# One core, attention and two expert stages: the dense stage's first turn by eight block products, and the groups' token numbers and shares kept in DRAM as rows

## The chip, the core and the metric

The kernel runs on one core of a Trainium2 chip. The metric is the device time of one execution in microseconds (us), the median of three runs. A profile is one further execution, recorded by the hardware.

A core has five queues of instructions, each worked off in order: TensorE (PE; its weight loads are shown apart as PEld), VectorE (DVE), ScalarE (ACT), GpSimd (POOL) and SyncE (SP), which here issues nearly all DMAs. They wait for each other through semaphores. An instruction that waits holds all that stands behind it on its engine.

## What is computed

```python
# attention: 4 batches, 8 heads, 576 tokens, 64 wide; causal, window of 128, linear bias
attn = softmax(q @ k.T / 8 + bias, masked) @ v              # -> x, 2304 tokens x 512
# first expert stage: 8 experts, each takes 288 tokens, greedily by the largest logit
logits = x @ w_gate                                         # 2304 x 8
for idx in argsort(-logits.flatten()): assign the token if it is free and the expert has room
for e in range(8): y[mask_e] = relu(x[mask_e] @ w1[e]) @ w2[e]        # 512 -> 1024 -> 512
# second, dense stage: 4 experts, every token through each
p = probs / (probs.sum(-1) + 1e-9)
out = sum(p[:, e] * (relu(y @ w1_e) @ w2_e) for e in range(4))
```

All is float32. A product of two float32 matrices is made of three PE passes over a high and a low part of each operand (`mm3`: high x high, high x low, low x high).

## The kernel before

**Attention** comes first, tokens in 18 tiles of 128. Its rows, with the token's four shares behind the 512 values, go to `x_dram`.

**The grouped stage** follows: eight groups g = 0 to 7 of 288 tokens. For each group a routing chain on DVE and PE (`count`, `enough`, `any`, `narrow`, six rounds, then `who` to `whole`) finds the expert and the token numbers `idx` (96 x 3); POOL gathers the tokens' rows from `x_dram` into `xg`; PE turns them (`rows`, tiles `tp`), and then multiplies by the expert's weights (`hp_a`, then `y`). The weights come in 16 pieces of 128 x 512 (`raw_a`), with five buffers: SP loads a piece (`load_piece`, L745), ACT rounds it to the high part (`wh_a`, L753), DVE makes the low part (`wl_a`, L758). While a group's own work runs, the routing of the next one is in progress, interleaved on DVE and PE. PE time that would be free is filled with a part of the dense stage, expert 0's first 768 hidden columns (`hp_f`, `po_f`, `pt`; partial sums go to `part_dram`).

The step `keep` (L946 to L950) stores a group's token numbers and its shares for later use: `id_dram` has one 4-byte number for each token and `p_dram` four shares, and both are written from tiles whose 96 partitions are tokens, so each token is a piece of its own. `shares_of` (L1035, L1040) reads shares back tile by tile for `pt`; after the last group `ids` and `pp` are read for the dense stage (L1269, L1271).

The order of this stage is set by `arranged` (L1207): each `step` has an engine, an assumed duration, its needs with lags and a rank, and a list scheduler puts them in an order that then is each engine's program order.

**The dense stage** makes 7 units of hidden columns for 3 pairs of token chunks (2 x 384 tokens), 21 turns. A turn's first matmul (512 deep) is cut in halves of depth, hidden columns and tokens, and done by seven products of sums of blocks in place of eight (`first_products`, L1303): x and w1 blocks are added and subtracted beforehand (`token_work`, L1095, on DVE: tiles `b`, `t`; `weight_work`, L1137, on POOL: tiles `a`, `s`) and each of the seven results split in high and low (`xh`/`xl`, `wh`/`wl`). The products land in PSUM tiles `m`; four of the results need further additions on DVE (`u`, `cs`, with a copy `s` by ACT). While the turn's products run, the second matmul of the turn before is interleaved (`po`, with weights `vh`, `vl` from `w2raw`), and the operands of the next turn are prepared; a number called slot says behind which product. The first turn has no turn before it: its operands are prepared at the end of the grouped stage (step `turn`, L1196) and no second matmul lies between its products. After `fctx` closes (L1264) only PE and ACT keep the written order; DVE, POOL and SP instructions of the dense stage are ordered by the framework's own scheduler.

Of the kernel before, what the change touches and what calls it, by code (L numbers as in the profile page):

```python
# [19 lines left out]
P = 128  # L20
# [5 lines left out]
def fused_kernel(ctx: ExitStack, tc: tile.TileContext, q, k, v, w_gate, w1, w2, probs, m2w1, m2w2, out, dbg=None):  # L26
# [25 lines left out]
    id_dram = dram.tile([NT, 1], I32, name="id_dram")  # L52
    p_dram = dram.tile([NT, E2], F32, name="p_dram")
# [470 lines left out]
    moe = ctx.enter_context(tc.tile_pool(name="moe", bufs=1))  # L524
    ps_y = ctx.enter_context(tc.tile_pool(name="ps_y", bufs=2, space=PSUM))
# [389 lines left out]
    for g in range(E):  # L915
# [29 lines left out]

        def keep(g=g):  # L946
            gs = slice(g * CAP, (g + 1) * CAP)
            nc.sync.dma_start(id_dram[gs, :].rearrange("(j i) o -> i (j o)", i=CB), grp[g]["idx"])
            nc.sync.dma_start(p_dram[gs, :].rearrange("(j i) e -> i j e", i=CB), grp[g]["xg"][:, :, DM:])
        step(("keep", g), SP_, 1.2, keep, [(("gather", g), 10.0), (("rows", g, NK - 1), 1.0)], 2)  # L950
# [80 lines left out]
        def shares_of(g=g):  # L1031
            p0 = g * CAP
            fill[g]["p"] = [fw.tile([P, E2], F32, tag="ppf", name=f"ppf_{g}_{t}", bufs=3) for t in range(FULL)]
            for t in range(FULL):
                nc.sync.dma_start(fill[g]["p"][t], p_dram[p0 + t * P : p0 + (t + 1) * P, :])  # L1035
            if g % GR == GR - 1:
                pr = fw.tile([P, E2], F32, tag="ppr", name=f"ppr_{g}")
                for j in range(GR):
                    r0 = (g - GR + 1 + j) * CAP + FULL * P
                    nc.sync.dma_start(pr[j * REM : (j + 1) * REM, :], p_dram[r0 : r0 + REM, :])  # L1040
                fill[g]["p"].append(pr)
# [53 lines left out]
    def token_work(pair):  # L1095

        raw, out, todo = {}, [None] * 7, []
# [17 lines left out]
        def split(i, a, needs):  # L1115
            def up():
                out[i] = [dp["w"].tile([P, 2, CH], F32R, tag=f"x{n}", name=f"x{n}{i}_{pair}", bufs=7) for n in "hl"]
# [3 lines left out]
            return len(todo) - 1  # L1121

# [11 lines left out]
        split(6, (1, 1), [t3])  # L1134
        return todo, out

    def weight_work(u, key):  # L1137
# [41 lines left out]
        l = {ik: load(*ik) for ik in ((0, 0), (1, 0), (1, 1), (0, 1))}  # L1179
# [16 lines left out]
    step(("turn",), SP_, 0.0, late_pools, [("first h", E - 1, NFF - 1, NK - 1), ("fl", E - 1, NFF - 1), ("out", E - 1), ("keep", E - 1), ("gather", E - 1)], 1)  # L1196
    first, begins, later = {}, [], []
    for what, (todo, made) in (("t", token_work(0)), ("w", weight_work(0, "0"))):
        first[what] = made
        begins += [(slot, i, what, todo) for i, (*_, slot) in enumerate(todo) if slot < 7]  # L1200
        later += [(slot, fn) for _, _, fn, _, slot in todo if slot >= 7]
    for n, (slot, i, what, todo) in enumerate(sorted(begins, key=lambda b: b[:3])):
        eng, us, fn, needs, _ = todo[i]
# [215 lines left out]
```

## Time and profile before

| | us |
|---|---|
| three runs | 1252.45, 1257.78, 1258.47 |
| median | 1257.78 |
| the profiled execution | 1262.0 |
| its span, first to last instruction | 1260.3 |
| attention, up to | about 157 |
| routing of the first group, up to | about 200 |
| grouped stage, up to | about 615 |
| change over to the dense stage, up to | about 655 |
| dense stage, up to | 1260.3 |

The profile has a page (busy time of each engine, the span in 40 slices, DMA queues, the chain that ended last, costliest groups of instructions) and a trace that can be asked for the instructions of a stretch in order of time. In these a row gives the start from the span's beginning, the duration, the engine, the line, the operation and its tiles; what stands in brackets is how long the engine had been idle just before and what released it. PEclk is the clock granted to TensorE: 1.00 is 2.4 GHz, 0.50 is 1.2 GHz.

### The profile page before, as it was taken

Reading aid. Unit: us, or ns where it says so; the run is one execution under the profiler, and the core shown is the slowest. Engines: PE = TensorE matmul, PEld = TensorE weight load, DVE = VectorE, ACT = ScalarE, POOL = GpSimd, SP = SyncE. Lnnn points to the kernel's source line nnn. Section 1 sums busy time; section 2 is a strip of 40 time slices with the busy share of each in tenths; the row PEclk is TensorE's granted clock in tenths of the full one; section 3 lists DMA queues with packets and bytes.
Section 4 is the critical chain, followed back from the end, with each engine's and each line's share of the span. In section 5 each row is a group of like instructions: output and inputs, shape, how many; then the busy total and the mean of one; then the engine's idle time right before and its main releaser. Section 6 shows DMA issues by size and latency. Waiting matters only on the chain.

```text
span 1260.3 us, 22074 instructions
## 1 busy us (share of the span) xinstructions
PE 1193.8 (95%) x7975; PEld 1078.0 (86%) x7975; DVE 786.2 (62%) x2048; ACT 525.1 (42%) x1284; POOL 516.8 (41%) x499
## 2 busy tenths in 40 slices
PE   7999926989999999999979999999999999999997
PEld 6998825979898899999968988888888898898886
DVE  6999887868887675442564544764444584454443
ACT  8998733333333334443443333333333342333320
POOL 8867601101000100000487766446664635676622
PEclk9999957989999999999989999999999999999999
DMA  9663144454454525651462322233222113232101
GB/s 180 147 148 85 44 151 112 121 110 132 105 113 101 139 86 145 117 150 20 143 211 59 100 67 68 63 104 118 68 59 59 51 43 109 60 100 68 51 25 51
DMA packets 140734, 122.29 MB, mean 97 GB/s; under 512 B 77648, under 2 KB 104784, under 8 KB 140624
## 3 DMA queue, kind: packets, MB, share of 16 engines
q1 hardware_dynamic: 137648, 111.40, 34.2%
q0 software_dynamic: 2976, 9.48, 2.3%
q8 instruction: 63, 1.03, 0.4%
q14 instruction: 47, 0.39, 0.1%
HBM read 101.88 MB, written 18.96 MB: 96 GB/s over the span
## 4 chain that ended last, share of the span: by engine, by line
PE 72%; DVE 6%; issue 4%; DMA 3%; POOL 2%; ACT 1%; SPq 0%; POOLq 0%; DVEq 0%
PE po L779 8%; PE po L780 8%; PE po L778 8%; PE m L780 7%; PE m L779 7%; PE m L778 7%; PE hp_a L778 3%; PE y L778 3%; PE hp_a L779 2%; PE hp_a L780 2%; PE y L780 2%; PE y L779 2%; DMA raw_a<-in_moe_w_dram 2%; PE hp_f L778 2%; PE hp_f L780 2%
## 5 line engine op out<-in xcount | busy, mean ns | idle before, releaser
L1292 DVE SCALAR_TENSOR_TENSOR acc<-po,pp,acc 128x512 f32<-128x512 f32 x126 | 94.4, 749 | 185.1 <-PE po L780 184.7
L778 PE MATMUL m<-xh,wh 128*128 128x384 f32 x546 | 184.6, 338 | 8.1 <-ACT s L1338 5.6
L780 PE MATMUL m<-xh,wl 128*128 128x384 f32 x546 | 185.8, 340 | 0.0
L779 PE MATMUL m<-xl,wh 128*128 128x384 f32 x546 | 185.7, 340 | 0.0
L779 PE MATMUL po<-vl,hh 128*128 128x512 f32 x468 | 185.2, 396 | 0.0
L780 PE MATMUL po<-vh,hl 128*128 128x512 f32 x468 | 185.2, 396 | 0.0
L778 PE MATMUL po<-vh,hh 128*128 128x512 f32 x468 | 184.7, 395 | 0.0
L1164 POOL TENSOR_TENSOR wl<-a,wh 128x512 fp32r<-128x512 f32 (+1 forms) x114 | 145.3, 1279 | 74.4 <-ACT wh L1162 74.2
L721 POOL DMA_INDIRECT xg<-x_dram,idx x24 | 25.1, 1045 | 362.9 <-PE hp_a L780 144.7
L787 ACT ACTIVATE hh<-cs 128x384 fp32r<-128x384 f32 x117 | 60.8, 525 | 205.4 <-DVE cs L1326 205.4
L1177 POOL TENSOR_TENSOR vl<-w2raw,vh 128x512 fp32r<-128x512 f32 x70 | 95.4, 1365 | 95.5 <-ACT vh L1174 95.5
L1162 ACT CAST wh<-a 128x512 fp32r<-128x512 f32 (+1 forms) x114 | 66.3, 583 | 142.3 <-POOL a L1155 91.6
L778 PEld LDWEIGHTS m<-xh,wh 128*128 128x128 f32 x546 | 104.0, 190 | 14.2 <-ACT s L1338 6.0
L779 PEld LDWEIGHTS m<-xl,wh 128*128 128x128 f32 x546 | 103.7, 190 | 5.7
L780 PEld LDWEIGHTS po<-vh,hl 128*128 128x128 f32 x468 | 87.9, 188 | 20.9
L780 PEld LDWEIGHTS m<-xh,wl 128*128 128x128 f32 x546 | 103.8, 190 | 0.0
L778 PEld LDWEIGHTS po<-vh,hh 128*128 128x128 f32 x468 | 87.8, 188 | 15.9
L779 PEld LDWEIGHTS po<-vl,hh 128*128 128x128 f32 x468 | 88.0, 188 | 15.7
L753 ACT CAST wh_a<-raw_a 128x512 fp32r<-128x512 f32 x128 | 73.5, 620 | 31.3 <-DMA raw_a<-in_moe_w_dram 31.2
L758 DVE TENSOR_TENSOR wl_a<-raw_a,wh_a 128x512 fp32r<-128x512 f32 x128 | 85.1, 681 | 1.3 <-ACT wh_a L753 0.3
L778 PE MATMUL hp_a<-xh,wh_a 128*128 128x288 f32 x256 | 81.8, 320 | 0.1
L790 DVE SCALAR_TENSOR_TENSOR hl<-cs,hh 128x384 fp32r<-128x384 f32 x117 | 73.8, 640 | 11.8 <-ACT hh L787 5.9
(241 smaller groups left out, 3047.6 us busy)
## 6 DMA issues: line engine op xcount, KB each, us to landing
raw_a<-in_moe_w_dram SPq DMA_DIRECT2D x128, 256.0 KB, 3.2
w2raw<-in_moe_w_dram SPq DMA_DIRECT2D x70, 256.0 KB, 2.7
a<-in_moe_w_dram SPq DMA_DIRECT2D x64, 256.0 KB, 3.1
x_dram<-x SPq DMA_DIRECT2D x18, 258.0 KB, 2.7
y_dram<-ys SPq DMA_DIRECT2D x8, 576.0 KB, 3.7
b<-y_dram SPq DMA_DIRECT2D x12, 384.0 KB, 4.3
acc<-part_dram SPq DMA_DIRECT2D x6, 768.0 KB, 5.8
k<-in_k_dram SPq DMA_DIRECT2D x16, 256.0 KB, 4.6
```

The costliest lines, as they stand in the source:

```text
L721: G.indirect_dma_start(out=xg[:, j, :], out_offset=None, in_=x_dram[:, :], in_offset=bass.IndirectOffsetOnAxis(ap=d["idx"][:, j : j + 1], ...
L753: S.copy(res[n][0][0][:, a, b], raw)
L758: V.tensor_tensor(lo[:, a, b], raw, hi[:, a, b].bitcast(F32), ALU.subtract)
L778: T.matmul(o, ah, bh, start=first, stop=False, **kept)
L779: T.matmul(o, ah, bl, start=False, stop=False, **kept)
L780: T.matmul(o, al, bh, start=False, stop=last, **kept)
L787: S.activation(h[0][:, f, :n], hp[:, :n], AF.Relu)
L790: V.scalar_tensor_tensor(h[1][:, f, :n], hp[:, :n], 0.0, h[0][:, f, :n].bitcast(F32), ALU.max, ALU.subtract)
L1162: S.copy(out[i][0], raw[a])
L1164: todo.append((POOL_, 1.3, lambda: G.tensor_tensor(out[i][1], raw[a], out[i][0].bitcast(F32), ALU.subtract), [len(todo) - 1], i))
L1177: todo.append((POOL_, 1.3, lambda: G.tensor_tensor(second[f][1], raw["w", f], second[f][0].bitcast(F32), ALU.subtract), [len(todo) - 1], 8 ...
L1292: V.scalar_tensor_tensor(accs[ch][:, i, :], po, pe, accs[ch][:, i, :], ALU.mult, ALU.add)
```

## The change

Two things change. **Rows in DRAM.** One DRAM tensor `kp_dram` with five rows (the token numbers and the four shares) takes the place of `id_dram` and `p_dram`. For each group ACT packs numbers and shares into a tile `pk` (96 x 15), PE turns it (`pkt`, 15 x 96), ACT copies it to `pks`, and one DMA writes 15 rows of 96 numbers. After the last group one DMA reads all back as 90 rows of 128 (`kt`), PE turns them (`ktt`), ACT copies them to `pp`, and DVE makes the whole numbers `ids` from it. `shares_of` reads one share for a token in place of four.

**The first turn.** For the first turn alone the seven products become eight, of plain blocks (`block_products`): four results, each a sum of two block products in one PSUM tile, so that no `s`, `u` or `cs` is made and only 4 + 4 blocks must be split before the turn. The sums of token blocks that the later turns of the pair need are made behind or during the turn; the sums of weight blocks are not made for this unit. The next unit's weights are prepared in earlier slots (`EARLY`). In later pairs one token operand moves from slot 5 to slot 6.

```diff
-    id_dram = dram.tile([NT, 1], I32, name="id_dram")
-    p_dram = dram.tile([NT, E2], F32, name="p_dram")
+    kp_dram = dram.tile([1 + E2, NT], F32, name="kp_dram")
...
+    pp = moe.tile([P, 1 + E2, NTL], F32, name="pp")
...
+        KR = (1 + E2) * NB
+        def pack(g=g):
+            pk = d["pk"] = rsm.tile([CB, 1 + E2, NB], F32, tag="pk", name=f"pk_{g}")
+            S.copy(pk[:, 0, :], d["idx"])
+            S.copy(pk[:, 1:, :].rearrange("p e j -> p j e"), d["xg"][:, :, DM:])
+        def packed_t(g=g):
+            grp[g]["pkt"] = ps_h.tile([P, 512], F32, tag="h", name=f"pkt_{g}")
+            T.transpose(grp[g]["pkt"][:KR, :CB], grp[g]["pk"].rearrange("p e j -> p (e j)"), ident[:CB, :CB])
+        def packed(g=g):
+            S.copy(grp[g]["pks"], grp[g]["pkt"][:KR, :CB])
         def keep(g=g):
-            nc.sync.dma_start(id_dram[gs, :].rearrange("(j i) o -> i (j o)", i=CB), grp[g]["idx"])
-            nc.sync.dma_start(p_dram[gs, :].rearrange("(j i) e -> i j e", i=CB), grp[g]["xg"][:, :, DM:])
-        step(("keep", g), SP_, 1.2, keep, [(("gather", g), 10.0), (("rows", g, NK - 1), 1.0)], 2)
+            nc.sync.dma_start(kp_dram[:, g * CAP : (g + 1) * CAP].rearrange("e (j i) -> e j i", i=CB), grp[g]["pks"])
+        step(("pack", g), ACT_, 0.5, pack, [(("gather", g), 10.0), (("rows", g, NK - 1), 1.0), (("keep", g - 1), 4.0) if g else None], 2)
+        step(("packed t", g), PE_, 0.2, packed_t, [("pack", g), ("rows", g, NK - 1), bank(banks_h, 4, ("packed", g))], 2)
+        step(("packed", g), ACT_, 0.25, packed, [("packed t", g), (("keep", g - 1), 4.0) if g else None], 1)
+        step(("keep", g), SP_, 0.6, keep, [("packed", g)], 2)
+        if g == E - 1:
+            def by_tiles():
+                nc.sync.dma_start(d["kt"], kp_dram.rearrange("e (t p) -> (e t) p", p=P))
+            def tiles_t():
+                T.transpose(grp[E - 1]["ktt"][:, :KRT], grp[E - 1]["kt"], ident[:KRT, :KRT])
+            def tiles():
+                S.copy(pp.rearrange("p e t -> p (e t)"), grp[E - 1]["ktt"][:, :KRT])
...
-                nc.sync.dma_start(fill[g]["p"][t], p_dram[p0 + t * P : p0 + (t + 1) * P, :])
+                nc.sync.dma_start(fill[g]["p"][t], kp_dram[1, p0 + t * P : p0 + (t + 1) * P].rearrange("(p o) -> p o", o=1))
...
+        if pair == 0:
+            l = {kj: load(*kj) for kj in ((0, 1), (1, 1), (0, 0), (1, 0))}
...
+            for i, kj in ((7, (0, 1)), (6, (1, 1)), (0, (0, 0)), (2, (1, 0))):
+                split(i, kj, [l[kj]])
+            todo[:] = [(*t[:4], 0) for t in todo]
+            t3 = less("t3", (1, 1), (0, 1), ALU.subtract, [], 7)
+            less((0, 1), (0, 1), (0, 0), ALU.subtract, [], 7)
+            less((0, 0), "t3", (0, 0), ALU.add, [], 7)
...
+        if key == "0":
+            for i, ik in ((0, (0, 0)), (2, (0, 1)), (3, (1, 0)), (5, (1, 1))):
+                split(i, ik, [l[ik]])
+            todo[:] = [(*t[:4], 0) for t in todo]
+            for f in range(nf):
+                second_piece(f)
+            return todo, (out, second)
...
-    nc.sync.dma_start(ids, id_dram.rearrange("(t p) o -> p (t o)", p=P))
-    nc.sync.dma_start(pp, p_dram.rearrange("(t p) e -> p t e", p=P))
+    V.tensor_copy(ids, pp[:, 0, :])
...
+    def block_products(u, pair, w, x, h, key):
+        wb = {(0, 0): w[0], (0, 1): w[2], (1, 0): w[3], (1, 1): w[5]}
+        xb = {(0, 0): x[0], (1, 0): x[2], (1, 1): x[6], (0, 1): x[7]}
+        for i, j, bank in ((0, 1, 1), (0, 0, 2), (1, 1, 3), (1, 0, 1)):
+            for f in range(nh):
+                for k in range(2):
+                    for c in range(2):
+                        mm3(m[:, :CH], a[0][:, c, fs], a[1][:, c, fs], b[0][:, c, :], b[1][:, c, :], k == c == 0, k == c == 1)
+                hid_up(m, h[j], i * nh + f, CH)
+                hid_lo(m, h[j], i * nh + f, CH)
...
+    EARLY = (0, 0, 0, 2, 2, 7, 7, 7, 8, 9, 10, 11, 12)
...
-                work += [(slot, fn) for _, _, fn, _, slot in todo]
+                work += [(EARLY[slot] if n == 0 else slot, fn) for _, _, fn, _, slot in todo]
...
-        for i, _ in enumerate(first_products(u, pair, w[0], x, h, str(n))):
+        for i, _ in enumerate((first_products if n else block_products)(u, pair, w[0], x, h, str(n))):
```

What the planner and the framework's scheduler make of it is seen in the order of instructions. The first place is SP in group 1, from the weight piece ahead of `keep` on (`idx` and `xg` are the group's numbers and gathered rows, `raw_a` weight pieces, `pt` partial sums).

Before:

```order
L745 DMA raw_a_1_1_0_5056<-in_moe_w_dram 128x512
L948 DMA id_dram<-idx_4828 96x3x1
L949 DMA p_dram<-xg_4837 96x3x4
L745 ISA
L745 DMA raw_a_1_2_0_5087<-in_moe_w_dram 128x512
L1070 DMA part_dram<-pt_0_5085 128x512
L745 ISA
L745 DMA raw_a_1_3_0_5115<-in_moe_w_dram 128x512
L1070 DMA part_dram<-pt_1_5147 128x512
```

After:

```order
L746 DMA raw_a_1_1_0_5059<-in_moe_w_dram 128x512
L965 DMA kp_dram<-pks_5081 5x3x96
L746 ISA
L746 DMA raw_a_1_2_0_5099<-in_moe_w_dram 128x512
L1107 DMA part_dram<-pt_0_5097 128x512
L746 ISA
L746 DMA raw_a_1_3_0_5124<-in_moe_w_dram 128x512
L1107 DMA part_dram<-pt_1_5159 128x512
```

Two DMAs became one, at the same place in front of the weight pieces 1_2 and 1_3.

The second place is ACT in the same group, from the last turned tile of tokens on (`tp`, `xh`).

Before:

```order
L937 CAST xh_5023<-tp_3_5047 128x288
L753 CAST wh_a_1_4966<-raw_a_1_2_0_4972 128x512
L753 CAST wh_a_1_4966<-raw_a_1_3_0_4997 128x512
L1063 ACTIVATE pt_0_5085<-po_f_0_4984,ppf_0_4475 128x512
L753 CAST wh_a_1_5096<-raw_a_1_0_0_5036 128x512
L753 CAST wh_a_1_5096<-raw_a_1_1_0_5056 128x512
L1063 ACTIVATE pt_1_5147<-po_f_1_5073,ppf_1_4476 128x512
```

After:

```order
L938 CAST xh_5022<-tp_3_5045 128x288
L953 CAST pk_5067<-idx_4832 96x3
L954 COPY pk_5067<-xg_4839 96x3x4
L754 CAST wh_a_1_4966<-raw_a_1_2_0_4964 128x512
L962 COPY pks_5081<-pkt_5076 15x96
L754 CAST wh_a_1_4966<-raw_a_1_3_0_4994 128x512
L1100 ACTIVATE pt_0_5097<-po_f_0_4999,ppf_0_4490 128x512
L754 CAST wh_a_1_5105<-raw_a_1_0_0_5043 128x512
L754 CAST wh_a_1_5105<-raw_a_1_1_0_5059 128x512
L1100 ACTIVATE pt_1_5159<-po_f_1_5092,ppf_1_4491 128x512
```

Three small instructions stand among the roundings `wh_a`; the third, `pks`, waits for PE's transpose `pkt`.

The third place is DVE at the change over, from the first low part of a token block on (`b`: token blocks as loaded, `t`: the difference t3, `m` and `mb`: results of products).

Before:

```order
L1120 TENSOR_TENSOR xl_0_9684<-b_0_9662,xh_0_9683 128x768
L1111 TENSOR_TENSOR t_0_9704<-b_0_9668,b_0_9672 128x768
L1111 TENSOR_TENSOR b_0_9672<-b_0_9672,b_0_9662 128x768
L1111 TENSOR_TENSOR b_0_9662<-t_0_9704,b_0_9662 128x768
L1120 TENSOR_TENSOR xl_0_9710<-b_0_9679,xh_0_9709 128x768
L1120 TENSOR_TENSOR xl_0_9733<-b_0_9672,xh_0_9732 128x768
L1120 TENSOR_TENSOR xl_0_9741<-b_0_9662,xh_0_9740 128x768
L1111 TENSOR_TENSOR b_0_9679<-b_0_9679,b_0_9662 128x768
L1120 TENSOR_TENSOR xl_0_9763<-t_0_9704,xh_0_9762 128x768
L1120 TENSOR_TENSOR xl_0_9785<-b_0_9679,xh_0_9784 128x768
L1120 TENSOR_TENSOR xl_0_9792<-b_0_9668,xh_0_9791 128x768
L1326 TENSOR_TENSOR u_0_0_9873<-m_0_0_9859,s_0_0_9838 128x384
```

After:

```order
L1161 TENSOR_TENSOR xl_0_9737<-b_0_9715,xh_0_9736 128x768
L1151 TENSOR_TENSOR t_0_9877<-b_0_9721,b_0_9715 128x768
L1151 TENSOR_TENSOR b_0_9715<-b_0_9715,b_0_9725 128x768
L1161 TENSOR_TENSOR xl_0_9749<-b_0_9721,xh_0_9748 128x768
L1161 TENSOR_TENSOR xl_0_9739<-b_0_9725,xh_0_9738 128x768
L1151 TENSOR_TENSOR b_0_9725<-t_0_9877,b_0_9725 128x768
L1161 TENSOR_TENSOR xl_0_9743<-b_0_9732,xh_0_9742 128x768
L1151 TENSOR_TENSOR b_0_9732<-b_0_9732,b_0_9725 128x768
L791 SCALAR_TENSOR_TENSOR hl_1_9846<-mb_0_0_9847,hh_1_9845 128x384
L791 SCALAR_TENSOR_TENSOR hl_1_9846<-mb_0_1_9862,hh_1_9845 128x384
L1161 TENSOR_TENSOR xl_0_9741<-b_0_9725,xh_0_9740 128x768
L791 SCALAR_TENSOR_TENSOR hl_0_9844<-mb_0_0_9909,hh_0_9843 128x384
```

Before, three subtractions and seven low parts stand ahead of `u`, the first use of a product. Now four subtractions and four low parts stand ahead of the results `hl`; two of the subtractions stand in front of the second low part.

## Rows read from the trace of the kernel before

**Rows 1.** Busy time by stage: engine busy us (instructions), then PEclk, DMA share, GB/s.

```profile
core 0: us, PE busy (x) PEld busy (x) DVE busy (x) ACT busy (x) POOL busy (x), PEclk, DMA share, GB/s
200.00:330.00 130.00, 119.41 (x915) 106.79 (x915) 103.35 (x328) 45.57 (x104) 7.21 (x6) 0.94 0.46 107
330.00:615.00 285.00, 284.62 (x2146) 265.21 (x2146) 168.32 (x463) 108.44 (x252) 14.36 (x15) 1.00 0.45 114
615.00:655.50 40.50, 32.36 (x144) 29.42 (x143) 32.88 (x30) 19.41 (x38) 34.80 (x25) 0.87 0.56 172
655.50:1200.00 544.50, 544.50 (x2698) 487.96 (x2697) 280.62 (x445) 187.74 (x367) 324.22 (x261) 1.00 0.25 75
```

**Rows 2.** PE in order of time, the two waits in groups 0 and 1.

```profile
219.66 0.20 PE L578 MATMUL ns<-sat,ones_bf 8*128 8x32 bf16 x1 [4.45 <-DVE sat L574]
275.83 0.19 PE L668 MATMUL pf<-mk,triu 128*128 128x36 bf16 x1 [4.77 <-DVE totb L657]
```

**Rows 3.** DVE in order of time, what stood ahead of those releases.

```profile
217.31 0.46 DVE L790 SCALAR_TENSOR_TENSOR hl_a<-hp_a,hh_a 128x288 fp32r<-128x288 f32 x1 [4.98 <-ACT hh_a L787]
274.53 0.46 DVE L790 SCALAR_TENSOR_TENSOR hl_a<-hp_a,hh_a 128x288 fp32r<-128x288 f32 x1 [5.53 <-ACT hh_a L787]
```

**Rows 4.** ACT in order of time, the same two stretches.

```profile
215.24 0.62 ACT L753 CAST wh_a<-raw_a 128x512 fp32r<-128x512 f32 x1 [5.85 <-DMA raw_a<-in_moe_w_dram]
273.57 0.62 ACT L753 CAST wh_a<-raw_a 128x512 fp32r<-128x512 f32 x1 [7.24 <-DMA raw_a<-in_moe_w_dram]
```

**Rows 5.** DMA issues, whole span: tiles, queue, count, KB each, median us to landing.

```profile
raw_a<-in_moe_w_dram SPq DMA_DIRECT2D x128, 256.0 KB, 3.2
id_dram<-idx SPq DMA_DIRECT2D x8, 1.1 KB, 11.3
p_dram<-xg SPq DMA_DIRECT2D x8, 4.5 KB, 11.2
ppr<-p_dram SPq DMA_DIRECT2D x8, 0.5 KB, 2.8
```

**Rows 6.** DMA issues from 201.5 to 209.5.

```profile
raw_a<-in_moe_w_dram SPq DMA_DIRECT2D x4, 256.0 KB, 13.0
```

**Rows 7.** Busy time while the clock was low, after three of the PE waits (columns as Rows 1).

```profile
219.80:223.30 3.50, 3.50 (x16) 3.37 (x15) 2.61 (x8) 0.25 (x1) 0.00 (x0) 0.56 0.02 5
276.10:280.70 4.60, 4.60 (x20) 4.60 (x20) 4.39 (x16) 0.45 (x2) 0.00 (x0) 0.50 0.26 73
649.60:652.70 3.10, 3.10 (x11) 3.10 (x10) 2.90 (x4) 1.80 (x5) 3.10 (x4) 0.50 0.73 199
```

**Rows 8.** PE in order of time, the first turn's products.

```profile
626.95 0.34 PE L778 MATMUL m<-xh,wh 128*128 128x384 f32 x1
...
630.94 0.34 PE L780 MATMUL m<-xh,wl 128*128 128x384 f32 x1
636.93 0.69 PE L778 MATMUL m<-xh,wh 128*128 128x384 f32 x1 [5.65 <-ACT s L1338]
...
648.56 0.45 PE L778 MATMUL m<-xh,wh 128*128 128x384 f32 x1 [2.49 <-DVE u L1326]
...
654.42 0.33 PE L778 MATMUL m<-xh,wh 128*128 128x384 f32 x1
```

**Rows 9.** DVE in order of time, token blocks.

```profile
616.68 1.46 DVE L1120 TENSOR_TENSOR xl<-b,xh 128x768 fp32r<-128x768 f32 x1 [1.16 <-ACT xh L1118]
618.06 2.05 DVE L1111 TENSOR_TENSOR t<-b,b 128x768 f32<-128x768 f32 x1
643.65 2.06 DVE L1111 TENSOR_TENSOR t<-b,b 128x768 f32<-128x768 f32 x1 [5.71 <-DMA b<-y_dram]
```

**Rows 10.** POOL in order of time, weight blocks.

```profile
617.30 2.00 POOL L1164 TENSOR_TENSOR wl<-a,wh 128x512 fp32r<-128x512 f32 x1
643.60 1.30 POOL L1177 TENSOR_TENSOR vl<-w2raw,vh 128x512 fp32r<-128x512 f32 x1
```

**Rows 11.** PE and ACT in order of time, the nearest to the new transposes and copies.

```profile
256.90 0.96 PE L931 MATMUL tp<-ident,xg 96*128 96x96 f32 x9
615.07 0.35 ACT L1028 CAST resth<-fhh 128x192 fp32r<-128x192 f32 x1
```

**Rows 12.** DMA of the second weights at the turn (issues from 619.85 to 620.5).

```profile
w2raw<-in_moe_w_dram SPq DMA_DIRECT2D x2, 256.0 KB, 2.9
```

## What I expect of the time

> **What bounds the kernel now.** I read the busy time by stage first [rows 1]. From 330 to 615 and from 655.5 to the end TensorE is busy for the whole of both stretches (284.62 of 285, 544.50 of 544.5) with the granted clock at 1.00: there only fewer passes would help, and the change takes none away. What can be regained lies in two places: the 200 to 330 stretch, groups 0 and 1 (PE 119.41 of 130), and the change over, 615 to 655.5 (32.36 of 40.5, clock 0.87). Then I read PE's waits in these two, and followed each back from releaser to releaser. Attention, the first routing (157 to 200) and the tail hold no line that the change touches, and I leave them as they are.
>
> In groups 0 and 1 PE waits 4.45 and 4.77 us for DVE [rows 2]. DVE had just waited 4.98 and 5.53 for ACT's `hh_a` [rows 3]; `hh_a` stands on ACT behind a rounding `wh_a` that had waited 5.85 and 7.24 for a weight piece [rows 4]. A piece lands 3.2 us after its issue as a rule [rows 5], but the four issued around the first `keep` took 13.0 [rows 6], and the two DMAs of `keep` itself take 11.3 and 11.2 for 1.1 and 4.5 KB [rows 5]: 288 pieces each, one per token. So the chain reads: many small pieces, late weight piece, late rounding, late low part, late routing step, idle PE. Behind each wait the clock is low [rows 7]: 3.5 us at 0.56 and 4.6 us at 0.50.
>
> In the change over the first turn waits 5.65 for ACT's copy `s` and 2.49 for DVE's `u` [rows 8], and the clock falls behind both; one such piece is 3.1 us at 0.50 [rows 7].
>
> **Term 1, `keep` as rows.** The two DMAs of 288 pieces become one of 15 pieces. Taken to land as the other small transfers do, 2.8 to 3.2 us [rows 5], it no longer holds the weight pieces back by 13.0 − 3.2 = 9.8 us; as that is more than ACT's waits of 5.85 and 7.24, these go, and with them the two PE waits. Worth: 4.45 + 4.77 of waiting, and of the low clock 3.5 × 0.44 = 1.5 and 4.6 × 0.50 = 2.3, together **13.0 us**. Groups 2 to 7 have the same DMAs and PE loses nothing there [rows 1], since PE's queue there holds enough other work; nothing is to be had from them.
>
> What comes next where the waits go? DVE, busy 103.35 of these 130 us [rows 1]. The same work in 117 us is 88%, so some steps of the routing will be late by a little. Bounds: 0, and half the gain, 6.5. I take **+2.0**, nearer the lower end, since PE at full in groups 2 to 7 stands beside a DVE at 168.32 of 285 and shows that filling works when DVE has slack, while here it has little.
>
> What it adds. PE gets nine transposes (eight `pkt`, one `ktt`). The nearest row is nine 96 × 96 transposes in 0.96 us, 0.11 each [rows 11]; one at half clock would be 0.2. So 1.0, with 2.0 as upper end: **+1.0**. ACT gets three small instructions in each group, at most 0.35 each by the conversion of 192 columns [rows 11], 8.4 us in all, beside PE: ACT is busy 45.57 of 130 and 108.44 of 285 [rows 1]. DVE gets one small conversion (`ids`), and loses nothing to it before the first `po`.
>
> The Trainium skill ("TensorE: Matmul & The Clock Gate", Part 4: PE-mode transpose) gives about 275 ns for a transpose in a kernel's context; the trace's nine back to back do not agree. By it the nine would cost 2.5 us (an estimate from that page) and the sum would come out 1.5 later.
>
> It also adds a loop between engines: PE's `pkt` waits for ACT's `pk`, ACT's `pks` for `pkt`. Behind `pks` on ACT stand `wh_a` roundings, for which `hp_a` waits on PE; behind `pkt` on PE stands all. In groups 1 to 7 nine passes of `po_f_0` stand between the last `tp` and `pkt`, about 2 us of cover against two copies of 0.35; in group 0 `pkt` stands right behind a routing product and I count the copies, **+0.5** (bounds 0 and 2.5, a wait as for `u`). Without the cover each group would pay what ACT is late. For `ktt` the read of `kp_dram` is issued about 9 us ahead of PE's place for it, where small DMAs take 3.
>
> **Term 2, the first turn.** It runs now from 626.95 to 654.42, 27.47 us [rows 8], for seven products of 12 passes. The 23 passes from 626.95 to 630.94 give 0.1735 us for one. Eight products are 96 passes, 16.6 us if nothing waits: **−10.8**. (The seven alone would be 14.6, so waits and clock cost 12.9 now; the eighth product gives 2.1 of it back.)
>
> Does anything wait? With the old start on DVE (616.68) and its old durations, 1.46 for a low part and 2.05 for a subtraction [rows 9], the new order ends: low part of block (0,1) 618.1, t3 620.1, subtraction 622.1, low part of (1,1) 623.6, of (0,0) 625, subtraction 627, low part of (1,0) 628.5. The products start at 626.95, 631.1, 635.3 and 639.4; the second is the first to need (1,0) and has 2.6 us in hand. POOL makes four low parts of weights at 2.00 [rows 10] from 617.3, so the last is there by about 625.5, with two products before its use. POOL, busy 34.80 of 40.5 [rows 1], loses four sums and three low parts, near 2 us each, and has room for the next unit's weights, which come earlier.
>
> The next wait is behind the turn. The first `po` comes some 1.1 us after 643.55 and needs all six low parts of results and the `vh`, `vl` of its weights. On DVE the last results stand behind a subtraction for the next pair, whose tile `b` comes by a DMA; in the old trace that subtraction had waited 5.71 for it [rows 9]. On POOL two of the four `vl`, 1.30 each [rows 10], come through two buffers `w2raw` whose loads take 2.9 [rows 12], and the last would end about 647.5, for the fourth step of `po`. I count **+1.0**; the lower end is 0, the upper two waits as for `u` with one low clock of 3.1 × 0.5: 6.5.
>
> **The sum**: −13.0 − 10.8 + 2.0 + 1.0 + 0.5 + 1.0 = −19.3 us. The profiled execution took 1262.0 (span 1260.3 and 1.7 around it), so 1242.7; it lies 4.2 above the median of the runs, 1257.78, and I forecast the median: 1238.5, rounded to **1238**.
>
> **Rivals.**
> 1. The rows bring nothing. Either the pieces behind the new DMA are still late, as the loads of `ppf` still have one piece per token, or DVE, at 88%, hands back each wait as another. For: DVE's share, and that DVE itself, not the weights, ends both waits by name [rows 2]. Against: both times DVE was idle for 5 us and more [rows 3], so it isn't its work that lacks time, and short DMAs of the old share loads (`ppr`) land in 2.8 [rows 5]. Then −10.8 + 1.0 + 1.5 = −8.3: **1249.5**.
> 2. The turn's gain is taken back: the second low part stands behind two subtractions, the tile `b` and the second weights come late, and a wait within or right behind the turn brings the low clock with it. For: at present each of the two waits did so. Against: the 2.6 us in hand. Price: 5.65 + 1.5 in place of the 1.0 counted, −13.15: **1244.6**; at worst all of term 2, near 1249.
> 3. Slower: the loop of PE and ACT. Where ACT stands at a `wh_a` that waits for its piece, `pk` or `pks` comes late, and PE stands at `pkt` with all behind it, in each of the eight groups. At a wait like the old ones, 4.6 and 1.9 of clock behind it, eight groups lose 52: **1290**. It decides from a mean loss of 2.4 us a group, where it has eaten the 19.3. For: ACT did wait for pieces 5.85 and 7.24 [rows 4]. Against: this comes from the DMAs that go, the other pieces land at 3.2, and where PE is full ACT is under 40% busy [rows 1].
>
> **How the numbers follow.** Forecast 0.71, rival 1 0.11, rival 2 0.13, rival 3 0.05. About 0.5%, 6.3 us, is what a measurement of this kernel can tell from no change; so faster means under 1251.5. The forecast and rival 2 lie wholly under it, of rival 1 about half, of rival 3 a light form of one or two groups: faster 0.89, same 0.07, slower 0.04. The range: with all additions at nothing the sum is −23.8, 1234, and the three runs spread 5.3 below their median, of which I take 4: low 1230. All additions at their upper end give 6.5 + 2.0 + 2.5 + 6.5 = 17.5, −6.3: 1251.5, which also takes in rivals 1 and 2: high 1251.
>
> **What would show it.** Right: pieces issued around `keep` land in some 3 us; no PE wait above 1 us and no clock under 1.00 in the two spots of groups 0 and 1; from the first product of blocks to the next turn's products one unbroken row of passes, the eight products in 16.6 us. Wrong: PE waiting for `pk` at `pkt`, for `kt` at `ktt`, or for a low part between the products of the turn; ACT waiting 5 us and more for a piece in the early groups; a new DVE wait in 200 to 317 as long as the old; the write of `kp_dram` landing as late as 11 us. What makes the forecast wrong most easily is a new wait that lasts long enough to bring the low clock, since that costs half of the 3 to 5 us behind it.

## The result, and the profile after

| | kernel before | changed kernel |
|---|---|---|
| runs (us) | 1252.45, 1257.78, 1258.47, 1261.27 | 1240.48, 1241.30, 1243.19, 1243.34 |
| median | 1258.12 | 1242.24 |
| profiled execution | 1262.0 (span 1260.3) | 1241.3 (span 1239.2) |

The ratio is 0.988, with a 95% interval of 0.9854 to 0.9906: 15.9 us faster by the medians. The forecast was 1238, range 1230 to 1251.

The busy time by stage of the changed kernel, to be laid beside [rows 1] (columns as there):

```profile
core 0: us, PE busy (x) PEld busy (x) DVE busy (x) ACT busy (x) POOL busy (x), PEclk, DMA share, GB/s
200.00:330.00 130.00, 128.09 (x1032) 114.03 (x1031) 111.09 (x357) 50.73 (x121) 9.10 (x9) 0.97 0.40 120
330.00:615.00 285.00, 282.20 (x2075) 261.69 (x2075) 167.62 (x441) 113.69 (x271) 18.27 (x16) 1.00 0.36 112
615.00:655.50 40.50, 39.51 (x203) 35.87 (x202) 22.34 (x28) 16.74 (x35) 29.70 (x26) 1.00 0.61 191
655.50:1200.00 544.50, 544.50 (x2714) 491.14 (x2713) 284.91 (x447) 187.69 (x367) 315.86 (x255) 1.00 0.24 72
```

PE is at work for 128.09 of 130 us where it was 119.41, and for 39.51 of 40.5 where it was 32.36. (The PEclk of 0.97 in the first row is its start: 0.50 from 200 to 206, where the kernel before has 0.52, and 1.00 from 208 on.) In 330 to 615 it is the other way round: 282.20 in place of 284.62. Two new waits there, 1.06 and 1.03, explain most of it. PE's rows in order of time, changed kernel:

```profile
366.73 0.18 PE L579 MATMUL ns<-sat,ones_bf 8*128 8x64 bf16 x1 [1.06 <-DVE sat L571]
...
420.94 0.18 PE L579 MATMUL ns<-sat,ones_bf 8*128 8x64 bf16 x1 [1.03 <-DVE sat L571]
...
617.60 0.33 PE L779 MATMUL mb<-xh,wh 128*128 128x384 f32 x1
...
634.24 0.33 PE L779 MATMUL m<-xh,wh 128*128 128x384 f32 x1
...
638.82 0.50 PE L780 MATMUL po<-vl,hh 128*128 128x512 f32 x1 [0.99 <-POOL vl L1246]
```

The first product starts at 617.60 where it was 626.95 [rows 8]: 9.35 us came out of what lies ahead of the turn. By the first turned tile `tp` of group 0 (198.93 before, 198.39 now) and of group 2 (315.42 and 303.67), 0.5 of this arose ahead of group 0 and 11.2 in groups 0 and 1, and 2.4 were lost again behind them. The eight block products run from 617.60 to 634.24, 16.64 us, with no gap, in place of the 27.47 [rows 8], and the only wait behind them is 0.99 for a `vl`.

From the first product to the start of the seventh `acc` (DVE's sum of the dense stage's results; at 682.30 before, 663.32 after) the profiled executions took 55.35 us before and 45.72 after, 9.6 less; from there to the end they took 2.1 less. 9.35 + 9.6 + 2.1 is the whole difference of the spans. The last of the three stands in no part of the prediction.

### The profile page after: what moved, and what is told of

Its sections match the earlier page's. It is cut to its first block, busy times and chain, and to the rows that moved or that the text cites. A ratio compares the mean times of both kernels' runs of the same rounds, so it can differ in the third digit from the quotient of the medians.

```text
span 1239.2 us, 22110 instructions
## 1 busy us (share of the span) xinstructions
PE 1186.3 (96%) x7996; PEld 1073.1 (87%) x7996; DVE 778.5 (63%) x2040; ACT 526.6 (42%) x1305; POOL 502.9 (41%) x492
## 3 DMA queue, kind: packets, MB, share of 16 engines
q8 instruction: 63, 1.03, 0.4%
## 4 chain that ended last, share of the span: by engine, by line
PE 75%; DVE 6%; issue 4%; POOL 1%; DMA 1%; ACT 0%; POOLq 0%; ACTq 0%; DVEq 0%
PE po L780 8%; PE po L781 8%; PE po L779 8%; PE m L781 7%; PE m L779 7%; PE m L780 7%; PE hp_a L779 3%; PE y L779 3%; PE hp_a L781 3%; PE hp_a L780 2%; PE y L781 2%; PE y L780 2%; PE hp_f L779 2%; PE po_f L779 2%; PE hp_f L781 2%
## 5 line engine op out<-in xcount | busy, mean ns | idle before, releaser
L1233 POOL TENSOR_TENSOR wl<-a,wh 128x512 fp32r<-128x512 f32 (+1 forms) x112 | 141.2, 1267 | 158.6 <-ACT wh L1231 140.0
L781 PE MATMUL m<-xh,wl 128*128 128x384 f32 x518 | 174.8, 337 | 0.0
L779 PE MATMUL m<-xh,wh 128*128 128x384 f32 x518 | 174.3, 336 | 0.0
L780 PE MATMUL m<-xl,wh 128*128 128x384 f32 x518 | 173.9, 336 | 0.0
L788 ACT ACTIVATE hh<-cs 128x384 fp32r<-128x384 f32 x111 | 57.9, 525 | 201.4 <-DVE cs L1401 201.4
L779 PEld LDWEIGHTS m<-xh,wh 128*128 128x128 f32 x518 | 97.4, 188 | 5.2
L779 PEld LDWEIGHTS po<-vh,hh 128*128 128x128 f32 x468 | 88.3, 189 | 15.2
L780 PEld LDWEIGHTS m<-xl,wh 128*128 128x128 f32 x518 | 97.2, 188 | 4.8
L781 PEld LDWEIGHTS m<-xh,wl 128*128 128x128 f32 x518 | 97.2, 188 | 0.0
```

What stands on the lines that cost most here:

```text
L779: T.matmul(o, ah, bh, start=first, stop=False, **kept)
L780: T.matmul(o, ah, bl, start=False, stop=False, **kept)
L781: T.matmul(o, al, bh, start=False, stop=last, **kept)
L788: S.activation(h[0][:, f, :n], hp[:, :n], AF.Relu)
L1233: todo.append((POOL_, 1.3, lambda: G.tensor_tensor(out[i][1], raw[a], out[i][0].bitcast(F32), ALU.subtract), [len(todo) - 1], i))
```

## The experiments

They ran later, on three chips: e1 to e4, e7 and e8 on one, c_before, c_after, e6 and w4 on another, e9 and e10 on the third. On which chip the first measurement ran is not recorded. Each was timed beside the kernel before, whose median in the four sessions was 1251.5 to 1252.4 us (runs from 1248.4 to 1257.3), 6 below the first measurement; the three chips do not differ in it.

| kernel | median us | ratio to before, 95% interval |
|---|---|---|
| changed kernel (c_after) | 1237.57 | 0.9879, 0.9858 to 0.9899 |
| rows alone (e1) | 1245.61 | 0.9947, 0.9930 to 0.9964 |
| blocks alone (e2) | 1243.38 | 0.9937, 0.9919 to 0.9955 |
| pieces in groups 0, 1 (e3) | 1241.46 | 0.9917, 0.9898 to 0.9936 |
| pieces in groups 2 to 7 (e4) | 1237.97 | 0.9889, 0.9870 to 0.9908 |
| pieces three times, 0, 1 (e6) | 1255.20 | 1.0022, 1.0008 to 1.0037 |
| pieces three times, 2 to 7 (e7) | 1242.16 | 0.9916, 0.9877 to 0.9955 |
| pieces three times, 0, 1, ACT's queue (e10) | 1254.69 | 1.0017, 0.9999 to 1.0035 |
| before with an unused tile (e8) | 1254.00 | 1.0017, 0.9995 to 1.0038 |
| before, tiles placed as after (e9) | 1250.54 | 0.9995, 0.9974 to 1.0016 |
| changed kernel, four `w2raw` (w4) | 1236.80 | 0.9877, 0.9858 to 0.9895 |

**The two parts apart.** e1 is the kernel before with all that the change does to `keep`, `shares_of`, `ids` and `pp`, and the first turn as it was. e2 is the kernel before with `block_products` and the changes of the turn's operands, `keep` as it was.

> The rows in DRAM alone: the token numbers and shares are packed, turned and written as 15 rows, as in the changed kernel; the first turn keeps its seven products with sums. Theory of the prediction: term 1 is independent of the turn, so about 9.4 us off the kernel before (the changed kernel's first product starts 9.35 earlier), near 1248.7 where before is 1258.1; PE's waits of 4.45 and 4.77 in groups 0 and 1 are gone, the two in the first turn, 5.65 and 2.49, still there. Rival, the two parts help only together (the shorter groups just move the same weight pieces and token loads closer to the turn, which then waits longer): less than 5 us off. A second forecast: the runs of before spread over 9 us (1252.5 to 1261.3), those of the changed kernel over 3; if the late pieces are what varies, this kernel spreads over about 3.

> The eight block products in the first turn alone; token numbers and shares go to DRAM as 288 pieces each in two DMAs, as before. Theory: 27.5 us of first turn become 16.6 and about 1 us of wait behind it, so about 9.7 us off, near 1248.4 where before is 1258.1; the waits of 4.45 and 4.77 in groups 0 and 1 stay. Rival, the parts overlap: the sum of this and of the rows alone would differ from what both give together, 15.9 us by the medians, by more than 4. The spread of its runs stays at 6 us or more, as the late pieces are still there.

PE's waits, the first two rows in e1, the other three in e2:

```profile
624.76 0.69 PE L779 MATMUL m<-xh,wh 128*128 128x384 f32 x1 [5.81 <-ACT s L1373]
635.66 0.55 PE L779 MATMUL m<-xh,wh 128*128 128x384 f32 x1 [2.44 <-DVE u L1361]
```

```profile
267.36 0.18 PE L668 MATMUL pf<-mk,triu 128*128 128x36 bf16 x1 [3.06 <-DVE totb L657]
274.80 0.28 PE L559 MATMUL cnt<-ge,oh 128*8 128x64 bf16 x4 [0.96 <-DVE oh L133]
638.70 0.51 PE L779 MATMUL po<-vl,hh 128*128 128x512 f32 x1 [0.98 <-POOL vl L1209]
```

The rows took 6.5 us off, the blocks 8.7. Each removed its own waits and left the other's. Their sum, 15.2, is within half a microsecond of what both give together in c_after, 14.7. By the times alone that difference is known to some 4 us only; the traces say it more closely. The first product starts at 614.22 in e1 and at 614.11 in c_after, and from it to the seventh `acc` e2 takes 45.82 us and c_after 45.94: the parts are independent, and the rival that they overlap is out. The rows gave 3 less than expected, because in these later runs the kernel before has less to lose: in e2, group 0 has no wait above 0.5 and group 1 has 3.06 and 0.96, not the 4.45 and 4.77 that were forecast to stay. And 2.1 of the 6.5 come from the dense stage (below), not from the waits. The forecast on the spread held for e1 (1244.7 to 1246.9) and not for e2, which spreads over 3.2 us and not over 6.

**The kernel before and the changed kernel again, side by side.** No edit.

> The kernel before, profiled beside the others. Theory, the difference between 1258 and 1252 lies in how long the weight pieces behind the old DMAs are late: PE's waits in groups 0 and 1, 4.45 and 4.77 in the first profile, are shorter here by about 4 to 6 us together with their low clock, and the first turn's two waits are what they were (5.65 and 2.49). Rival, the 6 us lie in the attention or in the dense stage: waits of groups 0 and 1 as long as before.

> The changed kernel again, beside the others on their chip, where the kernel before takes 1252 us and not 1258. Theory, the parts add up: the rows alone gave 6.5 us and the block products alone 8.7, so 15.2 off, near 1237 to 1238, and PE's two waits for sat (1.06 and 1.03 at 366.7 and 420.9 in its profile) belong to that one execution and are gone, as they are in the kernel with the rows alone, whose gather stands at the same place. Rival, the waits for sat belong to the changed kernel's order: 1240 and more, with the waits in the profile again.

The kernel before (one execution, 1251.75): ACT's waits for a weight piece in groups 0 and 1, to be laid beside [rows 4], and PE's in group 1 behind them, beside [rows 2]:

```profile
210.75 0.62 ACT L753 CAST wh_a<-raw_a 128x512 fp32r<-128x512 f32 x1 [2.04 <-DMA raw_a<-in_moe_w_dram]
264.57 0.62 ACT L753 CAST wh_a<-raw_a 128x512 fp32r<-128x512 f32 x1 [4.43 <-DMA raw_a<-in_moe_w_dram]
```

```profile
266.83 0.18 PE L668 MATMUL pf<-mk,triu 128*128 128x36 bf16 x1 [1.95 <-DVE totb L657]
274.27 0.19 PE L559 MATMUL cnt<-ge,oh 128*8 128x64 bf16 x1 [0.95 <-DVE oh L133]
```

The same instructions in the same order, and ACT waits 2.04 and 4.43 us where it had waited 5.85 and 7.24; PE 0, 1.95 and 0.95 where it had waited 4.45 and 4.77. The first product then starts at 616.93 in place of 626.95, and from there to the seventh `acc` it takes 55.06 us against 55.35. Of the 10 us between the two profiles of one kernel, 0.9 lie ahead of group 0 and 9.1 in groups 0 and 1, in these waits and the low clock behind them, which c_before does not have there. That is the place that was expected, and more than the 4 to 6 us. The first turned tile of groups 0 and 2 and the first product, in c_before and then in c_after:

```profile
198.00 0.42 PE L931 MATMUL tp<-ident,xg 96*128 96x96 f32 x1
...
305.41 0.25 PE L931 MATMUL tp<-ident,xg 96*128 96x96 f32 x1
...
616.93 0.34 PE L778 MATMUL m<-xh,wh 128*128 128x384 f32 x1
```

```profile
197.89 0.42 PE L932 MATMUL tp<-ident,xg 96*128 96x96 f32 x1
...
302.38 0.25 PE L932 MATMUL tp<-ident,xg 96*128 96x96 f32 x1
...
614.11 0.33 PE L779 MATMUL mb<-xh,wh 128*128 128x384 f32 x1
```

Groups 0 and 1 take 107.41 us in the one and 104.49 in the other: between these two executions the rows in DRAM are worth 2.9 us there, where between the first two profiles it was 11.2 (116.49 and 105.28). The changed kernel came to 1237.57, and its two waits for `sat` are gone: they belonged to one execution and not to its order.

**Are the small pieces the cause?** The changed kernel, with the two old DMAs put back in `keep`, into DRAM that nobody reads; in e3 and e4 once, in e6 and e7 three times over:

```diff
         def keep(g=g):
+            if g < 2:                       # e4, e7: g >= 2
+                nc.sync.dma_start(id2_dram[...], grp[g]["idx"])
+                nc.sync.dma_start(p2_dram[...], grp[g]["xg"][:, :, DM:])
             nc.sync.dma_start(kp_dram[...], grp[g]["pks"])
```

> The changed kernel, and in groups 0 and 1 alone also the two old DMAs of 288 pieces each (numbers and shares of the tokens, to DRAM that nobody reads), at the place of keep; all engines else have the same instructions in the same order. Theory, many small pieces on the queue make the weight pieces late: PE's waits of 4 to 5 us in both groups come back with their low clock, 8 to 13 us slower than the changed kernel, 1250 to 1255. Rival, the waits went because the planner put ACT's and PE's work in another order: same time as the changed kernel within 2 us.

> The changed kernel and in groups 0 and 1 the two old DMAs three times over (six DMAs of 288 pieces each), at the place of keep, all else the same. With them once the kernel took 1241.5 and PE waited 1.92 and 0.86 in group 1 and 0.49 in group 0. Theory, the pieces are worked off one after the other, and every further pair of 288 holds the weight pieces behind it by 6 to 10 us: the waits grow to over 10 us in each group, 15 to 35 us slower than the changed kernel. Rival, the pieces are no cause (they go beside the weight pieces, on engines that are free): within 3 us of the kernel with them once.

PE's two longest waits in e3, then ACT's for a weight piece in e6 and PE's behind them:

```profile
265.33 0.18 PE L671 MATMUL pf<-mk,triu 128*128 128x36 bf16 x1 [1.92 <-DVE totb L660]
272.64 0.25 PE L562 MATMUL cnt<-ge,oh 128*8 128x64 bf16 x3 [0.86 <-DVE oh L135]
```

```profile
216.31 0.62 ACT L756 CAST wh_a<-raw_a 128x512 fp32r<-128x512 f32 x1 [7.38 <-DMA raw_a<-in_moe_w_dram]
277.72 0.62 ACT L756 CAST wh_a<-raw_a 128x512 fp32r<-128x512 f32 x1 [10.61 <-DMA raw_a<-in_moe_w_dram]
```

```profile
218.87 0.20 PE L581 MATMUL ns<-sat,ones_bf 8*128 8x32 bf16 x1 [5.11 <-DVE sat L577]
279.99 0.19 PE L671 MATMUL pf<-mk,triu 128*128 128x36 bf16 x1 [8.60 <-DVE totb L660]
```

Once costs 3.9 us against c_after, less than the 8 to 13 expected; the waits are those of c_before (1.92 and 0.86 beside 1.95 and 0.95), and so is the time of groups 0 and 1, 107.33 beside 107.41. Three times costs 17.6, inside the 15 to 35 expected, though the waits, 5.11 and 8.60 on PE, stayed under the 10 us of that forecast. All other engines had their instructions in the changed kernel's order, so the new order is not what removed the waits; that the pieces are gone is. The chain of [rows 2 to 4] stands here again, made by nothing but the extra DMAs.

In e6, however, part of the delay is the issue and not the transfer. SP's three weight loads behind `keep` in group 0, in c_after, e3 and e6:

```profile
202.59 6.40 SPq L746 DMA_DIRECT2D raw_a<-in_moe_w_dram  x3
201.74 5.63 SPq L748 DMA_DIRECT2D raw_a<-in_moe_w_dram  x3
207.63 6.48 SPq L748 DMA_DIRECT2D raw_a<-in_moe_w_dram  x3
```

With the pieces once, the first of them is issued as early as without; with the pieces three times, 5 us later. So e3 prices the late transfer, and e6 prices both.

> The same two old DMAs added to the changed kernel, in groups 2 to 7 alone. Theory, where PE's queue is full late pieces cost nothing: PE's waits for weights stay at 0. Beside this it tells what the two new waits of 1.06 and 1.03 us (366.7 and 420.9 of the changed kernel, PE waiting for DVE's sat, which starts 1.6 us after the count it needs is done) come from: in the changed kernel POOL's gather runs just then, as it no longer has to wait for the old DMA of the shares to have read xg. If the gather is the cause, it is held some 10 us longer here, the two waits go, and the time is 0 to 2 us below the changed kernel's. If it is something else, they stay and the time is the same. Rival to both, pieces cost in every group: over 4 us slower.

> The changed kernel and in groups 2 to 7 the two old DMAs three times over. The same in groups 0 and 1 cost 17.6 us, with PE waits of 5.11 and 8.60. Theory, from group 2 on the routing runs a group ahead and PE has other work queued, so late weight pieces reach no PE wait: under 3 us above the changed kernel, 1237 to 1241. Rival, the pieces cost the same in every group: six groups at 5 to 9 us, 1268 to 1290.

PE's waits that are new in e7:

```profile
431.58 0.18 PE L581 MATMUL ns<-sat,ones_bf 8*128 8x32 bf16 x1 [1.73 <-DVE sat L577]
488.76 0.40 PE L781 MATMUL hp_a<-xh,wh_a 128*128 128x288 f32 x1 [1.07 <-DVE hl_a L793]
546.06 0.40 PE L781 MATMUL y<-hh_a,wh_a 128*128 128x288 f32 x1 [1.35 <-DVE yl L1039]
```

Once in groups 2 to 7 costs 0.4 us, nothing that can be told. Three times costs 4.6 in six groups, more than the 3 that the theory allowed and far from the rival's 30, where in two groups it cost 17.6. The prediction's reading of [rows 1], that nothing is to be had there, is right, but the slack is not without end. On the waits for `sat` e4 tells nothing: they are missing in c_after as well. I had put them down to POOL's gather. In c_after the gather runs beside `sat` just as it did, and `sat` starts as soon as its count is done. That reading falls, and what delayed `sat` in the first profile stays open.

**Is it the queue?** e6 with the six DMAs of a group issued by ACT (`nc.scalar.dma_start`).

> The changed kernel and in groups 0 and 1 the two old DMAs three times over, as before, but issued by ACT on its own queue; the weight pieces stay on SP's. On SP's queue they cost 17.6 us. Theory, the pieces hold what stands behind them in the same queue: the weight pieces are free of them, and only ACT's six issues in each group are left, 1237 to 1242. Rival, the pieces take the 16 DMA engines from all queues alike: near 1255, PE's waits 5 and 8.6.

ACT in e10: in group 0 behind its own issues, in group 1 for weight pieces that SP had issued; then PE's waits:

```profile
210.69 0.41 ACT L790 ACTIVATE hh_a<-hp_a 128x288 fp32r<-128x288 f32 x1 [8.67 <-DMA kp_dram<-pks]
...
273.90 0.62 ACT L756 CAST wh_a<-raw_a 128x512 fp32r<-128x512 f32 x1 [7.63 <-DMA raw_a<-in_moe_w_dram]
278.69 0.62 ACT L756 CAST wh_a<-raw_a 128x512 fp32r<-128x512 f32 x1 [3.87 <-DMA raw_a<-in_moe_w_dram]
```

```profile
213.56 0.20 PE L581 MATMUL ns<-sat,ones_bf 8*128 8x32 bf16 x1 [3.63 <-DVE sat L577]
276.16 0.19 PE L671 MATMUL pf<-mk,triu 128*128 128x36 bf16 x1 [5.28 <-DVE totb L660]
```

1254.69, as on SP's queue (1255.20): the other queue was no way out, and the theory that only what stands behind in the same queue is held is wrong. SP's loads in group 1, and two of SP's waits (in all, times, longest):

```profile
261.11 0.36 SPq L748 DMA_DIRECT2D raw_a<-in_moe_w_dram  x1
269.72 0.33 SPq L748 DMA_DIRECT2D raw_a<-in_moe_w_dram  x1
```

```profile
SPq L1114 <- DMA kp_dram<-pks: 7.6, 1, 7.6
SPq L748 <- DMA id_dram<-idx: 7.1, 1, 7.1
```

Two things are at work. The transfer is late on the other queue too: ACT's 7.63 end at 273.90 with the piece that SP had issued at 261.11, 12.8 us earlier, where 3.2 is the rule [rows 5]. And issues are held: the 3.87 end with the piece issued at 269.72, behind a DMA for which SP had waited 7.6 until the write `kp_dram` had landed; in group 0 a weight load of SP waited 7.1 for ACT's `id_dram` to land, and ACT did no other work for 8.67 while it issued its DMAs, the last of which waited for SP's `kp_dram`. In the trace each of these three waits for the completion semaphore that it is to use itself, and that the earlier DMA still had. So in this program the two queues are not independent in their issue either; how the 17 us divide between the two was not tried.

**The 2.1 us of the dense stage.** From the seventh `acc` to the last `po` the kernels with rows (e1, e3, e4, e6, e7, e10, c_after, w4 and the changed kernel) take 569.5 to 569.6 us, those without (before twice, e2) 571.6. PE has no wait there in any of them.

```diff
 # e8: one more tile where the changed kernel has pp, never read
+    pad = moe.tile([P, 5, NTL], F32, name="pad")
 # e9: pp itself there, as large as in the changed kernel; its later place is empty
+    pp5 = moe.tile([P, NTL, 1 + E2], F32, name="pp")
+    pp = pp5[:, :, :E2]
...
-    pp = moe.tile([P, NTL, E2], F32, name="pp")
```

> The kernel before with one unused tile of 360 bytes a partition (filled once by POOL) at the place where the changed kernel allocates pp, so that all tiles allocated later lie at other addresses. From the seventh acc to the end of the last po the kernels with the rows take 569.55 us, those without 571.64, whatever the first turn is, at the same instructions on PE. Theory, it is where the tiles lie: 569.5 here, and 2 us off the kernel before. Rival, it is the other form of pp (shares of one expert side by side) that DVE's acc reads, or the loads of numbers and shares that are gone: 571.6.

> The kernel before with pp allocated early and as large as in the changed kernel (360 bytes a partition, in place of 288 late), so that the later tiles lie where they lie in the changed kernel; all else as before. Theory, the time of PE's passes in the dense stage goes with the place of the tiles (571.64 us from the seventh acc to the last po in the kernel before, 572.40 with the unused tile, 569.55 with the rows): 569.55 here. Rival, it goes with the shares' form or the loads that the rows removed: 571.64.

The seventh `acc` and the last pass of `po`, in c_before, in e9 and in c_after:

```profile
671.99 0.75 DVE L1292 SCALAR_TENSOR_TENSOR acc<-po,pp,acc 128x512 f32<-128x512 f32 x1 [1.77 <-PE po L780]
1243.23 0.40 PE L780 MATMUL po<-vh,hl 128*128 128x512 f32 x1
```

```profile
672.92 0.75 DVE L1293 SCALAR_TENSOR_TENSOR acc<-po,pp,acc 128x512 f32<-128x512 f32 x1 [1.76 <-PE po L782]
1242.07 0.40 PE L782 MATMUL po<-vh,hl 128*128 128x512 f32 x1
```

```profile
660.05 0.75 DVE L1367 SCALAR_TENSOR_TENSOR acc<-po,pp,acc 128x512 f32<-128x512 f32 x1 [1.76 <-PE po L781]
1229.19 0.40 PE L781 MATMUL po<-vh,hl 128*128 128x512 f32 x1
```

To the end of the last pass: 571.64, 569.55 and 569.54. e9 computes and moves what the kernel before does; only the place of the later tiles is the changed kernel's (and `pp` itself lies elsewhere, with wider rows, which DVE reads and PE does not), and with it alone the 2.1 us are gone. e8, which shifts them by another amount, took 572.40, which neither theory expected, and says the same: the place matters, in both directions. This is shown by the traces, one of each kernel; the times of e8 and e9 (intervals of some 5 us) are too wide to tell 2 us. PE's groups from 700 to 1190, one row of `po` from c_before and one from c_after; e9 has 393 as well (the mean ns of one pass stands last before the idle time):

```profile
L779 PE MATMUL po<-vl,hh 128*128 128x512 f32 x374 | 148.0, 396 | 0.0
```

```profile
L780 PE MATMUL po<-vl,hh 128*128 128x512 f32 x375 | 147.5, 393 | 0.0
```

These means are of durations, and the passes overlap. From the start of a pass to the start of the next, a pass of `po` takes 231.3 ns in c_after in place of 233.2 in c_before, and one of the first matmul 175.2 in place of 175.0 (means over the 2824 passes from the seventh `acc` on): `po` is where the 2.1 us come from. Which tiles must lie where for that was not tried.

**The wait behind the turn.** The changed kernel with four buffers for `w2raw` in place of two.

> The changed kernel with four buffers for the second weights w2raw in place of two, so that all four loads of the first turn's second matmul are issued up front. Theory, PE's wait of 0.99 at the first steps of po is the fourth load's, which waits for a buffer: the wait goes, 1 us off, 1236 to 1237 if the changed kernel is at 1237.5. Rival, another input of that step (the low part behind a subtraction for the next pair) is next in line: same time.

PE at the same place in w4:

```profile
632.89 0.50 PE L780 MATMUL po<-vl,hh 128*128 128x512 f32 x1 [0.28 <-POOL vl L1246]
```

The wait falls from 0.86 (c_after) to 0.28; from the first product to the seventh `acc` it takes 44.99 us against 45.94. The buffer was the cause. The runs, 1234.7 to 1237.2 against 1235.8 to 1238.0, overlap, so the gain of about 1 us is shown by the trace and not by the times.

## Why the prediction came out as it did

**The bound, and term 1.** Right in its mechanism: small pieces, late weight pieces, late rounding, late routing, idle PE (e3, e6), and nothing in groups 2 to 7 (e4). In size, the first profile bears it out: 9.35 us to the first product, where the prediction had 13.0 − 2.0 − 1.0 − 0.5 = 9.5. In the later pair it was 2.8 (616.93 and 614.11): the waits that the 13.0 priced were those of one execution. And how the 9.5 was made is not how the 9.35 came about:

- The new waits of DVE in 200 to 330, counted at 2.0 because DVE would be 88% busy, did not come: DVE was 85% busy (111.09 of 130), and PE's longest wait there is 0.50, one that the kernel before had as well. What was lost was lost later, in two waits that the next profile does not have. The 2.0 was right by accident.
- The transposes were counted at 1.0 from the mean of nine in a row [rows 11]. Eight of them cost about 0.3 together, and the ninth, in group 0, is told below. The 275 ns of the Trainium skill ("TensorE: Matmul & The Clock Gate", Part 4: PE-mode transpose) are near the duration of one, 0.25, and not what PE loses by it. Two rows of the changed kernel, where the next pass starts 0.03 us after the start of the transpose:

```profile
473.60 0.25 PE L958 MATMUL pkt<-ident,pk 96*15 96x96 f32 x1
473.63 0.48 PE L779 MATMUL po_f<-wh_b,fhh 128*128 128x512 f32 x1
```

- At `pkt` in group 0, counted at 0.5, PE waited 0.14 for `pk`; the next pass starts 0.68 us after `pkt`, and 0.36 of this it waits for its own weight piece. Rival 3 did not come: in the other seven groups PE does not wait for `pk` at all.
- [rows 5] has the 3.2, which the prediction took for a small transfer beside the 2.8, for the weight pieces of 256 KB. No term of the sum hangs on it.

**Term 2.** Right step by step: eight products in 16.64 us where 16.6 was worked out, no wait among them, and 0.99 behind them where 1.0 was counted, for the `vl` that was named. 9.6 of the 9.8 expected, 9.1 in the later pair.

**The step that failed** is the last of the sum: the profiled execution "lies 4.2 above the median of the runs", so 4.2 came off the result too. That holds an execution's excess for a constant of the machine. c_before shows that it is not: one and the same kernel had its first product at 626.95 or at 616.93, and 9.1 of these 10 us lie in groups 0 and 1. The profiled execution was slower than each of the four runs of before, and by c_before what it had too much lay, for the most part, in the very waits that the change takes away (the four runs themselves were not profiled); the changed kernel has no such excess to carry (its profiled run is 0.9 below its median). In the prediction's terms, term 1 priced the waits of a slow execution, and the subtraction then took their excess off a second time. Without the subtraction the sum read 1242.7, and 1242.24 was measured; that the two lie so close is luck, since 2.1 us of the measured gain stand in no term. Put otherwise, the gain by medians, 15.9, is smaller than the 19.3 worked out from that profile and the 20.7 between the two profiled executions.

**What the prediction lacked** is the place of the tiles, 2.1 us in the dense stage, where it said that the change takes nothing away. Without it the forecast would have missed by 6 us and not by 4.

**Rivals.** 1 and 2 did not happen; none of the new waits (0.99 to 1.06) brought the low clock, of which the prediction was most afraid. The range held, and its upper end was needed for none of its cases.

## What to carry to other kernels

A wait behind a DMA of many small pieces differs from execution to execution (here 116.5 us for groups 0 and 1 in one profile of a kernel, 107.4 in another): take its price from several executions, and where a change removes it, don't carry the profiled run's excess over into the forecast. Writing one long row for each quantity, at the price of a transpose that hides among other passes, removed the wait. That it removes the spread of the times too is not shown: e2, with the old pieces, spread over 3.2 us, and the changed kernel over 2 to 3. And a change of a few hundred bytes early in the memory can move a stage that it never touches; where a stage has no waits and yet gets faster, look at the time of one pass.

## What the runs showed of the hardware that was not expected

- The time of the same matmul passes depended on where tiles lie: 571.64 us in the dense stage of the kernel before, 572.40 with 360 bytes a partition placed ahead (e8), 569.55 with the tiles where the changed kernel has them (e9).
- Six DMAs of 288 pieces in each of two groups cost as much when they were issued on ACT's queue as on SP's (1254.69 and 1255.20): a 256 KB load on SP's queue landed 12.8 us after its issue, and issues on either queue waited for landings on the other (7.1 us and more).
- Not each wait of 2 to 3 us lowered the clock. Behind 2.49 in the first turn it was 0.50 [rows 7], and behind the 1.84 of e8 at 214.76 too (0.50 from 216 to 219); behind the 3.06 of e2 it stayed at 1.00. The busy time in e2 from just behind that wait (columns as in [rows 1]):

```profile
267.00:269.00 2.00, 1.64 (x12) 1.51 (x12) 1.86 (x10) 0.67 (x3) 0.00 (x0) 1.00 0.63 229
269.00:271.00 2.00, 2.00 (x17) 2.00 (x16) 1.93 (x5) 0.41 (x1) 0.00 (x0) 1.00 0.24 54
```
